# Attention and gated MLP on one core: zero rows under the score operands of the first two pairs of heads

## The chip, the cores and the metric

The kernel runs on one core of a Trainium2 chip. The metric is the time of one execution in device microseconds; a kernel's figure is the median of its runs. The engines are called as the profile calls them: PE (TensorE, its matmuls), PEld (TensorE's weight loads), DVE (VectorE), ACT (ScalarE), POOL (GpSimd), SP (SyncE, whose queue issues nearly all transfers).

## The reference

For 8 batches of 8 heads, with 576 positions and 64 numbers per head, in float32:

```
scores = q @ k^T / 8 + cum[i] - cum[j]     # cum = cumsum(log(clip(f, 1e-4, 1)))
scores = -1e9 above the diagonal
attn   = softmax(scores);  a = attn @ v    # x = heads of a, side by side: 576 x 512 per batch
h      = relu(x @ w_in)                    # 512 -> 1024;  u, v = halves of h
v_n    = layer norm of v over its 512 columns
v_s    = w_spatial @ v_n + b_spatial       # over the 576 positions
out    = (u * v_s) @ w_out                 # 512 -> 512
```

w_in and w_out come as float64, all else as float32.

## The kernel before, in words

Heads are handled in pairs, P = 0 to 31, four pairs to a batch. One pair's attention is: scores, row by row of 128 queries (`scores`, and `scores_tail` for the last 64 queries of both heads); softmax, in which DVE takes the score out of PSUM with the mask and the minimum (L264, L285), ACT takes the exponential (L266, L290), DVE makes the reciprocal of the sums (L269, L270) and POOL multiplies by it (L274, L297); transposes on PE (L320, L333) with a copy out of PSUM; and the product with v (`attend`). The scores of pair P+1 are written between the steps of pair P. After every batch comes its gated MLP (`moe`), interleaved with the attention of later batches.

The scores need q, k and the decay. For the first four pairs (NQ = 4) they are plain float32 products: one tile per head, in the code `ta`, in traces `tf`, of 66 rows by 1216 columns. Columns 0 to 639 are the queries (stationary side), 640 to 1215 the keys (moving side). Rows 0 to 63 are q and k, loaded from memory (L220); rows 64 and 65 are the decay rows, which the kernel computes at its start (`decay_rows`) and copies over by a DMA (L221). There are two such buffers. From pair 4 on, q and k are split in two parts each, in tiles `ta` of 128 rows and `tb` of 68.

At the start PE runs 26 matmuls on `zm[:, 0:128]` and `zm[:, 0:512]`, a part of the mask tile that holds only zeros, into an unused PSUM tile. Meanwhile f is loaded, and DVE, ACT and POOL compute the decay rows (`ft`, `r`, `rt`). Then the weights: `load64` turns float64 into two float32 parts, per piece one ACT operation (L141), five on DVE (L142, L144, L145, L147, L148), two on POOL (L149, L151) and a copy on ACT (L150). `load_first` does four pieces of 512 columns beside the attention of pair 0 and loads w_spatial; `load_rest` does 8 pieces of 256 for w_in, and later 8 for w_out.

The order of each engine's instructions is set at build time by a scheduler that works from the code's order, the dependences and its own costs; each engine and each queue then works strictly in that order. PSUM holds three score tiles (`p0s`) during the first stage.

Of the kernel before, what the change touches and what calls it, by code (L numbers as in the profile page):

```python
# [8 lines left out]
F32 = mybir.dt.float32  # L9
# [9 lines left out]
BIG = 1.0e9  # L19
NF = 5  # L20
NQ = 4
LEAD = 0.25
S = 576
D = 64
# [5 lines left out]
QK = 640 + S  # L30
# [3 lines left out]
def f32(ap):  # L34
    return ap.bitcast(F32)
# [3 lines left out]
def attn_gmlp_kernel(ctx: ExitStack, tc: tile.TileContext, qk, v, f, w_in, w_sp, b_sp, w_out, out):  # L39
# [12 lines left out]
    wk = ctx.enter_context(tc.tile_pool(name="wk", bufs=1))  # L52
# [4 lines left out]
    V, A, G, T, SY = nc.vector, nc.scalar, nc.gpsimd, nc.tensor, nc.sync  # L57
# [139 lines left out]
    def mm(o, l, r, st, sp):  # L197
        T.matmul(o, l, r, start=st, stop=sp)  # L198
# [3 lines left out]
    def split(P):  # L202

        if P < NQ:
            return
# [9 lines left out]
    def prep(P, h):  # L215

        p = slice(64 * h, 64 * h + 64)
        if P < NQ:
            ta = wk.tile([66, QK], F32, name="tf", tag="ta", bufs=2)
            SY.dma_start(out=ta[0:64, :], in_=qk[P, p, :])  # L220
            last['dma', P, h] = SY.dma_start(out=ta[64:66, :], in_=r0s[0][32 * h + P:32 * h + P + 1])  # L221
            tab[P, h] = (ta,)
            return
        hi, lo = parts[P]
        ta = wk.tile([128, QK], F32R, name="ta", tag="ta", bufs=2)
        tb = wk.tile([128, QK], F32R, name="tb", tag="tb", bufs=2)
        SY.dma_start(out=f32(ta[0:64, :]), in_=hi[p, :])
        SY.dma_start(out=f32(ta[64:128, 0:640]), in_=lo[p, 0:640])
        SY.dma_start(out=f32(ta[64:128, 640:QK]), in_=hi[p, 640:QK])
        SY.dma_start(out=f32(tb[0:64, 0:640]), in_=hi[p, 0:640])  # L230
        SY.dma_start(out=f32(tb[0:64, 640:QK]), in_=lo[p, 640:QK])
        SY.dma_start(out=f32(tb[64:68, :]), in_=rows_v[:, P, h, :])
        tab[P, h] = (ta, tb)
# [12 lines left out]
    def qkt(o, P, h, q0, k0, n, first, final):  # L246

        k0 += 640
        ts = tab[P, h]
        for t in ts:  # L250
            r = 66 if len(ts) == 1 else 128 if t is ts[0] else 68
            mm(o, t[0:r, q0:q0 + 128], t[0:r, k0:k0 + n], first and t is ts[0], final and t is ts[-1])

    def scores(P, h):

        nm = wk.tile([128, 4], F32, name="nm", tag="nm", bufs=3)
        sm = wk.tile([128, 4], F32, name="sm", tag="sm", bufs=3)
        for i in range(NB):
            n = 128 * (i + 1)
            q0 = 128 * i  # L260
            sc = PS['s'].tile([128, 512], F32, name="sc")
            qkt(sc[:, 0:n], P, h, q0, 0, n, True, True)
            t = tt[h][:, TOFF[i]:TOFF[i] + n]
            V.tensor_tensor_reduce(out=t, in0=sc[:, 0:n], in1=zm[:, 640 - n:640], scale=-0.125, scalar=3.0e38,  # L264
                                   op0=ALU.add, op1=ALU.min, accum_out=nm[:, i:i + 1])
            last["exp", P, h, i] = A.activation(t, t, AF.Exp, bias=nm[:, i:i + 1], scale=-1.0,  # L266
                                                accum_out=sm[:, i:i + 1])
            yield 2 * max(107, 0.42 * n)
        V.tensor_scalar(out=sm, in0=sm, scalar1=1.0e-9, scalar2=None, op0=ALU.add)  # L269
        V.reciprocal(sm, sm)  # L270
        for i in range(NB):
            n = 128 * (i + 1)
            t = tt[h][:, TOFF[i]:TOFF[i] + n]
            G.tensor_scalar(out=t, in0=t, scalar1=sm[:, i:i + 1], scalar2=1.0, op0=ALU.mult, op1=ALU.mult)  # L274
        yield 0

    def scores_tail(P):
        nm = wk.tile([128, 4], F32, name="nm", tag="nm", bufs=3)
        sm = wk.tile([128, 4], F32, name="sm", tag="sm", bufs=3)
        for j in range(2):  # L280
            k0 = 288 * j
            sc = PS['s'].tile([128, 512], F32, name="sc")
            for h in range(2):
                qkt(sc[:, 0:288], P, h, 512, k0, 288, h == 0, h == 1)
            V.tensor_tensor_reduce(out=tl[:, k0:k0 + 288], in0=sc[:, 0:288],  # L285
                                   in1=zm[:, 0:288] if j == 0 else zm[:, 640:928], scale=-0.125, scalar=3.0e38,
                                   op0=ALU.add, op1=ALU.min, accum_out=nm[:, j:j + 1])
            yield 492
        V.tensor_tensor(out=nm[:, 2:3], in0=nm[:, 0:1], in1=nm[:, 1:2], op=ALU.min)
        A.activation(tl[:, 0:S], tl[:, 0:S], AF.Exp, bias=nm[:, 2:3], scale=-1.0, accum_out=sm[:, 0:1])  # L290
        V.tensor_scalar(out=sm[:, 0:1], in0=sm[:, 0:1], scalar1=1.0e-9, scalar2=None, op0=ALU.add)
        V.reciprocal(sm[:, 0:1], sm[:, 0:1])
        if P >= NF:
            G.tensor_scalar(out=tl[:, S:640], in0=tl[:, TL:S], scalar1=sm[:, 0:1], scalar2=1.0,
                            op0=ALU.mult, op1=ALU.mult)
        if True:
            G.tensor_scalar(out=tl[:, 0:S], in0=tl[:, 0:S], scalar1=sm[:, 0:1], scalar2=1.0,  # L297
                            op0=ALU.mult, op1=ALU.mult)
        yield 0
# [76 lines left out]
    def attention(b, ws=None):  # L376
        for P in range(b * PPB, (b + 1) * PPB):
            if P == 0:
                r0s.append(decay_rows())
                for h in range(2):  # L380
                    prep(0, h)

                warm = ps_a.tile([128, 512], F32, name="x0")
                for _ in range(26):
                    mm(warm, zm[:, 0:128], zm[:, 0:512], True, True)
                split_rows(ws, r0s[0])
                split(1)
                yield from scores(0, 0)
                yield from scores_tail(0)
                yield from scores(0, 1)  # L390
            nxt = P + 1 < NPAIR
            prep_v(P)
            if nxt:
                prep(P + 1, 0)
                prep(P + 1, 1)
# [166 lines left out]
    for b in range(B):  # L562
        gm = moe(b)
        dm, mon = 0.0, True
        while mon:
            while da < min(B, b + 1 + LEAD + dm):
                if not on:
# [46 lines left out]
```

## Time and profile before

| | |
|---|---|
| median of 3 runs | 815.69 us (813.99 to 815.85) |
| profiled execution | 813.26 us, of which the span from the first to the last instruction is 811.5 us |
| mean granted TensorE clock | 0.985 |

A time in the trace is counted from the start of the span. "[2.59 <-DVE nm L264]" behind a row means that the engine sat idle for 2.59 us before it, until DVE's work on `nm` at line 264 was done. "66*128 66x512" on a matmul is the stationary operand (66 rows, 128 columns) and the moving one. A float32 matmul is recorded as two.

### The profile page before, as it was taken

What the parts mean: (1) busy time and instruction counts of PE and PEld (TensorE: products, weight loads), DVE (VectorE), ACT (ScalarE), POOL (GpSimd) and SP (SyncE); (2) the same over time, 40 slices, a digit from 0 to 9 for tenths busy, and PEclk for the clock granted to TensorE, in tenths of its full rate; (3) what the DMA queues carried; (4) which work ended last, traced back from release to release, by engine and by line L of the source; (5) the groups of instructions that cost most, each with busy time, mean ns of one, the idle gap of its engine ahead of it and who ended that gap; (6) DMA issues with size and microseconds to landing.
All of it is one profiled execution on the core that took longest, in us unless ns stands there. A gap on an engine that the chain in (4) does not pass through costs nothing.

```text
span 811.5 us, 15566 instructions
## 1 busy us (share of the span) xinstructions
PE 788.3 (97%) x4980; PEld 704.9 (87%) x4980; DVE 567.1 (70%) x1726; ACT 535.2 (66%) x1432; POOL 478.1 (59%) x677
## 2 busy tenths in 40 slices
PE   7999899999999999999999999999999999999997
PEld 3676678998899989998799989999899988999996
DVE  5879989676976668766776668776786658765321
ACT  5587668676776667666686667776687657764431
POOL 4767788655766647555775537566675547643151
PEclk8699999999999999999999999999999999999999
DMA  7547754456545554565554565556554664430001
GB/s 201 143 121 208 197 140 116 120 151 165 139 122 135 135 146 117 128 166 140 125 141 112 150 152 126 123 144 151 131 130 107 163 164 111 95 77 14 27 1 66
DMA packets 47476, 103.50 MB, mean 128 GB/s; under 512 B 6961, under 2 KB 15153, under 8 KB 47330
## 3 DMA queue, kind: packets, MB, share of 16 engines
q1 hardware_dynamic: 47074, 101.98, 49.8%
q8 instruction: 40, 0.66, 0.3%
q10 hardware_dynamic: 320, 0.52, 0.3%
q14 instruction: 42, 0.34, 0.1%
HBM read 39.41 MB, written 10.68 MB: 62 GB/s over the span
## 4 chain that ended last, share of the span: by engine, by line
PE 87%; DVE 5%; POOL 2%; ACT 2%; DMA 2%; issue 1%; SPq 0%; ACTq 0%; POOLq 0%; DVEq 0%
PE ps L198 47%; PE sc L198 16%; PE x L198 12%; PE tp L320 8%; PE tp L198 2%; PE tp L333 2%; DMA out_dram<-o 1%; POOL tt L274 1%; DVE w L145 1%; ACT tt L266 1%; DVE tt L264 1%; DVE eh L342 0%; DVE wa L142 0%; DVE ef L305 0%; DMA w<-in_dram 0%
## 5 line engine op out<-in xcount | busy, mean ns | idle before, releaser
L274 POOL TENSOR_SCALAR tt<-tt,sm 128x128 f32<-128x128 f32 (+3 forms) x256 | 138.3, 558 | 94.7 <-DVE sm L270 86.4
L264 DVE CUSTOM_DVE_ANT_0 tt<-sc,zm 128x128 f32<-128x128 f32 (+3 forms) x256 | 122.4, 485 | 82.4 <-PE tp L320 63.0
L309 ACT CAST eh<-tp 128x512 fp32r<-128x512 f32 (+1 forms) x270 | 111.5, 425 | 87.2 <-PE tp L320 52.5
L266 ACT ACTIVATE tt<-tt,nm 128x128 f32<-128x128 f32 (+3 forms) x256 | 144.4, 565 | 26.5 <-DVE nm L264 21.5
L310 DVE TENSOR_TENSOR el<-tp,eh 128x512 fp32r<-128x512 f32 (+1 forms) x270 | 127.9, 485 | 25.0 <-ACT eh L309 22.8
L320 PE MATMUL tp<-ident,tt 128*128 128x128 f32 x640 | 113.7, 280 | 1.3 <-DVE ef L305 0.6
L198 PE MATMUL sc<-ta 128*128 128x128 f32 (+1 forms) x336 | 107.8, 327 | 3.9 <-DVE nm L264 3.8
L198 PE MATMUL x<-eh,vt 128*128 128x320 f32 (+4 forms) x378 | 104.5, 287 | 2.7 <-POOL vt L243 1.8
L198 PE MATMUL sc<-tb 68*128 68x128 f32 (+1 forms) x336 | 104.6, 316 | 0.0
L212 POOL TENSOR_TENSOR lo<-raw,hi 128x640 fp32r<-128x640 f32 (+1 forms) x56 | 83.2, 1506 | 18.5 <-ACT hi L210 18.4
L505 POOL TENSOR_TENSOR gl<-u,gh 128x256 fp32r<-128x256 f32 x64 | 47.2, 738 | 79.3 <-ACT gh L504 76.1
L198 PE MATMUL x<-el,vt 128*128 128x256 f32 x324 | 93.4, 306 | 0.0
L320 PEld LDWEIGHTS tp<-ident,tt 128*128 128x128 f32 x640 | 76.8, 142 | 10.9 <-ACT ef L305 1.2
L198 PEld LDWEIGHTS x<-eh,vt 128*128 128x128 f32 x378 | 71.2, 189 | 5.8 <-POOL vt L243 2.7
L198 PE MATMUL ps<-sph,vnh 128*128 128x256 f32 (+1 forms) x240 | 73.3, 306 | 0.2 <-ACT o L530 0.2
L198 PE MATMUL ps<-sph,vnl 128*128 128x256 f32 (+1 forms) x240 | 71.4, 298 | 0.0
L198 PEld LDWEIGHTS sc<-ta 128*128 128x128 f32 x336 | 63.5, 189 | 9.1 <-DVE nm L264 4.9
L198 PE MATMUL ps<-spl,vnh 128*128 128x256 f32 (+1 forms) x240 | 71.2, 296 | 0.0
L198 PE MATMUL ps<-xh,winh 128*128 128x256 f32 (+1 forms) x232 | 70.1, 302 | 0.1
L198 PE MATMUL ps<-xl,winh 128*128 128x256 f32 (+1 forms) x232 | 68.9, 297 | 0.0
L368 ACT CAST xh<-x 64x256 fp32r<-64x256 f32 (+1 forms) x128 | 49.8, 392 | 28.4 <-PE x L198 26.9
L198 PE MATMUL ps<-xh,winl 128*128 128x256 f32 (+1 forms) x232 | 68.4, 295 | 0.0
(190 smaller groups left out, 2127.8 us busy)
## 6 DMA issues: line engine op xcount, KB each, us to landing
raw<-in_dram SPq DMA_DIRECT2D x28, 608.0 KB
ta<-hi SPq DMA_DIRECT2D x56, 304.0 KB
vraw<-in_dram SPq DMA_DIRECT2D x32, 320.0 KB
tb<-hi SPq DMA_DIRECT2D x56, 160.0 KB
ta<-lo SPq DMA_DIRECT2D x56, 160.0 KB
out_dram<-o SPq DMA_DIRECT2D x32, 256.0 KB
ta<-hi SPq DMA_DIRECT2D x56, 144.0 KB
tb<-lo SPq DMA_DIRECT2D x56, 144.0 KB
```

Source lines behind the costliest of these rows:

```text
L145: V.scalar_tensor_tensor(out=w, in0=hi, scalar=0xC0000000, in1=a, op0=ALU.bitwise_and, op1=ALU.bitwise_or)
L198: T.matmul(o, l, r, start=st, stop=sp)
L212: G.tensor_tensor(out=lo[:, c], in0=raw[:, c], in1=f32(hi[:, c]), op=ALU.subtract)
L264: V.tensor_tensor_reduce(out=t, in0=sc[:, 0:n], in1=zm[:, 640 - n:640], scale=-0.125, scalar=3.0e38, op0=ALU.add, op1=ALU.min, accum_out=n ...
L266: last["exp", P, h, i] = A.activation(t, t, AF.Exp, bias=nm[:, i:i + 1], scale=-1.0, accum_out=sm[:, i:i + 1])
L274: G.tensor_scalar(out=t, in0=t, scalar1=sm[:, i:i + 1], scalar2=1.0, op0=ALU.mult, op1=ALU.mult)
L309: A.copy(h_ap, ps)
L310: V.tensor_tensor(out=l_ap, in0=ps, in1=f32(h_ap), op=ALU.subtract)
L320: T.transpose(out=tp[:, (i - c) * 128:(i - c + 1) * 128], in_=tt[h][:, TOFF[i] + 128 * c:TOFF[i] + 128 * c + 128], identity=ident)
L333: T.transpose(out=tp[:, j * 128:(j + 1) * 128], in_=tl[:, c * 128:(c + 1) * 128], identity=ident)
L368: last[P, h] = A.copy(hi, ps[m0:m0 + 64, 0:n])
L505: G.tensor_tensor(out=gl[j][:, 0:256], in0=g[:, 0:256], in1=f32(gh[j][:, 0:256]), op=ALU.subtract)
```

## The change

For pairs 0 and 1 (NPAD = 2) the score tile gets 128 rows in place of 66; DVE sets rows 64 to 127 to zero before the decay rows are copied into 64 and 65, and the matmuls take all 128 rows. Pairs 2 and 3 have 128 rows allotted as well, but use 66 as before.

```diff
+NPAD = 2
...
         if P < NQ:
-            ta = wk.tile([66, QK], F32, name="tf", tag="ta", bufs=2)
+            ta = wk.tile([128, QK], F32, name="tf", tag="ta", bufs=2)
+            if P < NPAD:
+                V.memset(ta[64:128, :], 0.0)
             SY.dma_start(out=ta[0:64, :], in_=qk[P, p, :])
             last['dma', P, h] = SY.dma_start(out=ta[64:66, :], in_=r0s[0][32 * h + P:32 * h + P + 1])
...
         for t in ts:
-            r = 66 if len(ts) == 1 else 128 if t is ts[0] else 68
+            r = (128 if P < NPAD else 66) if len(ts) == 1 else 128 if t is ts[0] else 68
```

Lines of the changed kernel stand one to three higher than before (L264 is L267, L142 is L143). The four memsets change the schedule of the first third of the program; behind about a third of each engine's list the two programs have the same order.

On DVE, at the program's start, before: the decay rows are finished (the scan at L103, the copy at L89), then two operations of the first weight piece come ahead of the first score (L264).

```order
L97 MEMSET ones 64x576
L100 TENSOR_SCALAR ft<-ft 64x576
L85 MEMSET r_114 32x2x64 x2
L103 SCALAR_TENSOR_TENSOR r_114<-ones,ft 64x576
L89 COPY r_114<-r_114 64x512
L85 MEMSET rt 32x4x64 x2
L142 TENSOR_SCALAR wa<-wa 128x512
L144 TENSOR_SCALAR wa<-wa 128x512
L264 ISA tt_94,nm<-sc,zm 128x128
```

The same place in the changed kernel (L104 is the scan, L267 the first score):

```order
L98 MEMSET ones 64x576
L222 MEMSET tf 64x1216 x2
L101 TENSOR_SCALAR ft<-ft 64x576
L86 MEMSET r_114 32x2x64 x2
L86 MEMSET rt 32x4x64 x2
L104 SCALAR_TENSOR_TENSOR r_114<-ones,ft 64x576
L90 COPY r_114<-r_114 64x512
L267 ISA tt_94,nm<-sc,zm 128x128
L267 ISA nm 128x1
L267 ISA tt_94,nm<-sc,zm 128x256
L267 ISA nm 128x1
L143 TENSOR_SCALAR wa<-wa 128x512
```

Two memsets came in behind the first; the memsets of `rt` moved ahead of the scan; and the first two scores moved ahead of the first weight operation, which was ahead of them before.

Further on, on DVE, where the scores of pair 0 end (`tl` is the tail of the queries, `sm` the sums of the softmax, `tt_95` the second head), before:

```order
L285 ISA tl,nm<-sc,zm 128x288
L285 ISA nm 128x1
L285 ISA tl,nm<-sc,zm 128x288
L285 ISA nm 128x1
L264 ISA tt_95,nm<-sc,zm 128x128
L264 ISA nm 128x1
L269 TENSOR_SCALAR sm<-sm 128x4
```

and in the changed kernel:

```order
L288 ISA tl,nm<-sc,zm 128x288
L288 ISA nm 128x1
L148 TENSOR_SCALAR wa<-w_179 128x512
L222 MEMSET tf 64x1216
L272 TENSOR_SCALAR sm<-sm 128x4
L145 TENSOR_SCALAR wa<-wa 128x512
L288 ISA tl,nm<-sc,zm 128x288
L288 ISA nm 128x1
L267 ISA tt_95,nm<-sc,zm 128x128
```

The memset for pair 1's first head and a weight operation now stand between the two halves of the tail. The memset of its second head stands in the same way behind the last score of `tt_95`.

On SP, the transfers for pair 1 and the third and fourth weight piece (`w_342` and `w_410`), before:

```order
L137 DMA w_265<-in_dram 128x1024
L113 DMA rows_d<-rt 64x4864
L232 DMA tb<-rows_d 4x1216
L220 DMA tf<-in_dram 64x1216
L221 DMA tf<-r_114 2x1x1216
L137 DMA w_342<-in_dram 128x1024
L137 DMA w_410<-in_dram 128x1024
L220 DMA tf<-in_dram 64x1216
```

and in the changed kernel (`w_346` and `w_414` are the same two pieces):

```order
L138 DMA w_269<-in_dram 128x1024
L114 DMA rows_d<-rt 64x4864
L223 DMA tf<-in_dram 64x1216
L235 DMA tb<-rows_d 4x1216
L224 DMA tf<-r_114 2x1x1216
L138 DMA w_346<-in_dram 128x1024
L223 DMA tf<-in_dram 64x1216
L224 DMA tf<-r_114 2x1x1216
L138 DMA w_414<-in_dram 128x1024
```

The fourth weight piece moved behind both transfers of pair 1's second head, and each L224 now waits for that buffer's memset, with the weight pieces queued behind it.

## The prediction and its working

> **What bounds the kernel now.** I read the page's engine totals, slices and chain first, then the busy times by stretch, then PE, DVE and SP in order of time over the first 40 us.
>
> ```profile
> span 811.5 us, 15566 instructions
> PE 788.3 (97%) x4980; PEld 704.9 (87%) x4980; DVE 567.1 (70%) x1726; ACT 535.2 (66%) x1432; POOL 478.1 (59%) x677
> ...
> PEclk8699999999999999999999999999999999999999
> ...
> PE 87%; DVE 5%; POOL 2%; ACT 2%; DMA 2%; issue 1%; SPq 0%; ACTq 0%; POOLq 0%; DVEq 0%
> ```
>
> PE is busy for 97% of the span and makes 87% of the chain that ended last. The clock is full but for the first two slices of 20 us, and there lies everything that the change touches.
>
> ```profile
> 10.00:20.00 10.00, 7.41 (x18) 4.48 (x17) 5.88 (x19) 5.20 (x14) 1.80 (x2) 0.62 0.80 217
> 20.00:30.00 10.00, 10.00 (x25) 6.08 (x24) 8.40 (x31) 7.03 (x21) 7.25 (x10) 0.50 0.61 170
> 36.00:40.00 4.00, 3.38 (x18) 2.26 (x17) 3.44 (x13) 1.96 (x5) 2.58 (x3) 0.96 0.69 212
> 40.00:60.00 20.00, 20.00 (x103) 14.76 (x102) 15.39 (x53) 16.24 (x45) 14.16 (x18) 1.00 0.42 117
> 60.00:100.00 40.00, 35.31 (x172) 24.98 (x171) 37.70 (x121) 28.14 (x82) 31.31 (x42) 1.00 0.77 200
> 140.00:811.00 671.00, 661.24 (x4391) 612.62 (x4390) 451.22 (x1386) 442.30 (x1185) 374.91 (x539) 1.00 0.49 121
> ```
>
> The columns are length, then PE, PEld, DVE, ACT, POOL, granted clock. There are four stages: to 36 us PE runs without a pause at half clock; from 40 to 60 it is the bound at full clock while DVE idles 4.6 us; from 60 to 100 DVE is the bound (37.7 of 40); from 140 on PE is at 98.5%. What the first stage gains therefore stays gained if DVE's list too is further along at 60 us: a lead of PE alone would be lost to the third stage.
>
> **Why the clock is low.** The first rows are PEld's and PE's in order of time.
>
> ```profile
> 5.18 0.15 PEld L198 LDWEIGHTS <-zm 128*128 128x128 bf16 x1 [0.28 <-issue]
> 5.60 3.34 PEld L198 LDWEIGHTS <-zm 128*128 128x128 bf16 x16 [0.27 <-issue]
> ...
> 9.61 1.54 PE L198 MATMUL sc<-tf 66*128 66x128 f32 x6 [0.18 <-DMA tf<-r]
> 13.74 11.46 PE L198 MATMUL sc<-tf 66*128 66x512 f32 x22 [2.59 <-DVE nm L264]
> ...
> 28.19 5.75 PE L198 MATMUL sc<-tf 66*128 66x512 f32 x10
> ...
> 33.95 1.06 PE L198 MATMUL x<-ef,vraw 128*128 128x256 f32 x2
> 34.80 1.27 PE L333 MATMUL tp<-ident,tl 128*128 128x128 f32 x5
> 35.87 0.60 PE L198 MATMUL x<-ef,vraw 128*128 128x128 f32 x2
> 36.73 0.63 PE L320 MATMUL tp<-ident,tt 128*128 128x128 f32 x4 [0.26 <-DVE ef L305]
> ```
>
> The weight loads of the opening matmuls start 0.42 us apart until 5.60 and then 0.21 apart (3.34 over 16): all-zero operands of 128 rows brought the clock up within 3.8 us of the first. PE then idles for 2.59 us before 13.74, the clock falls, and through 20 us of unbroken, mostly 66-row matmuls it does not rise; it does at 36.3 (0.96 over the four us from 36), after 2.4 us of 128-row work from 33.95 on. So 66 rows seem not to count as full activity, and zeros do count.
>
> The Trainium skill, page "TensorE: Matmul & The Clock Gate", section "What's actually happening", speaks against the change: the gate opens on how busy PE has recently been, after some 3.4 us of sustained work, and rows are not mentioned. By that alone the clock would have risen near 17 us, and padding would change nothing (the last rival below). Its two states agree with the 0.50 and 1.00 of the rows; the 20 us do not agree with its opening rule.
>
> **The matmuls themselves** cost the same with 128 rows.
>
> ```profile
> 43.86 0.39 PE L198 MATMUL sc<-tf 66*128 66x128 f32 x2
> 44.08 0.39 PE L198 MATMUL x<-ef,vraw 128*128 128x128 f32 x2
> ```
>
> Equal columns, 66 and 128 rows, 0.39 us both: I price the padding on PE at nothing. No instruction is added to PE or SP; four memsets are added to DVE.
>
> **The memsets.** The nearest rows are DVE's memsets at the start, the next rows its pace later.
>
> ```profile
> 0.90 0.54 DVE L97 MEMSET ones<- 64x576 f32 x1 [0.90 <-PEq L600]
> 3.51 0.81 DVE L100 TENSOR_SCALAR ft<-ft 64x576 f32<-64x576 f32 x1 [2.07 <-DMA ft<-in_dram]
> 5.07 1.35 DVE L103 TENSOR_TENSOR_SCAN r<-ones,ft 64x576 f32<-64x576 f32 x1 [0.39 <-ACT ft L101]
> 6.95 0.63 DVE L85 MEMSET rt<- 32x256 f32 x2
> 12.59 0.43 DVE L142 TENSOR_SCALAR wa<-wa 128x512 f32<-128x512 f32 x1 [5.01 <-ACT wa L141]
> ...
> 14.88 0.42 DVE L147 TENSOR_SCALAR wa<-w 128x512 uint32<-128x512 uint32 x1
> 15.22 0.55 DVE L264 CUSTOM_DVE_ANT_0 tt<-sc,zm 128x384 f32<-128x384 f32 x1
> ...
> 16.03 0.68 DVE L264 CUSTOM_DVE_ANT_0 tt<-sc,zm 128x512 f32<-128x512 f32 x1
> ...
> 16.64 0.69 DVE L148 SCALAR_TENSOR_TENSOR wa<-w,wa 128x512 f32<-128x512 uint32 x1
> 17.24 0.68 DVE L145 SCALAR_TENSOR_TENSOR w<-w,wa 128x512 uint32<-128x512 uint32 x1
> ...
> 34.74 1.64 DVE L148 SCALAR_TENSOR_TENSOR wa<-w,wa 128x512 f32<-128x512 uint32 x1
> ```
>
> 256 elements take 0.315 us and 576 take 0.54, so 1216 take 1.0 at that slope, 1.14 in proportion; I take 1.05. The two memsets of pair 0 run from 1.44 to 3.54, inside the 2.07 us in which DVE waits for f. If f came sooner they would cost up to 2.1. What does cost is the reordering behind them: the memsets of `rt` now precede the scan and need POOL's memset of `rt`.
>
> ```profile
> 3.96 1.47 POOL L82 MEMSET rt<- 64x1280 f32 x1
> ```
>
> That ends at 5.43, so the scan starts near 6.06 instead of 5.07. The decay rows, the first score (9.61) and, behind the decay rows on SP, the first weight load come 1.0 us later.
>
> The two memsets of pair 1 stand in DVE's list where it is busy: 2.1 us. Had they the stretch that a two-source operation shows (1.64 for 0.69), they would cost up to 5.0; at least 2.0.
>
> **The first stage, as DVE's list.** The mark is the copy and the score (L305, L264) that DVE reaches at 36.51, behind which PE starts its transposes at 36.73. From 13.39 to 36.51 are 23.1 us. Nominal cost by start-to-start distances in the rows above: 11 scores 4.3 (0.61 for 512, 0.47 for 384, down to 0.21), two tails 0.8, 10 one-source weight operations at 0.34 = 3.4, 8 two-source ones at 0.60 = 4.8, copies 0.7, small ones 0.7: 14.7. Of the rest, 4.3 are waits and 4.1 are operations that took longer than nominal.
>
> ```profile
> DVE tl L285 <- PE sc L198: 1.5, 1, 1.5
> ...
> DVE w L145 <- POOL winl L151: 1.1, 1, 1.1
> DVE tt L264 <- PE sc L198: 0.9, 1, 0.9
> ...
> DVE wa L142 <- POOL w L149: 0.6, 1, 0.6
> ```
>
> 2.4 of the waits are for PE at half clock, 1.7 for POOL.
>
> In the changed order, the first two scores leave PSUM before the weight piece arrives, so the 2.59 us gap of PE goes. DVE's dense work starts when ACT has the first piece:
>
> ```profile
> 11.90 0.66 ACT L141 ACTIVATE wa<-w 128x512 f32<-128x512 f32 x1 [1.14 <-DMA w<-in_dram]
> ...
> 20.26 2.69 SPq L137 DMA_DIRECT2D w<-in_dram  x2
> ...
> 21.65 2.48 POOL L274 TENSOR_SCALAR tt<-tt,sm 128x128 f32<-128x128 f32 x4 [0.61 <-DVE sm L270]
> ```
>
> 11.90 + 1.0 for the later load and 0.66 on ACT is 13.55. Up to the same mark the list lacks the first two scores (-0.55) and six weight operations, three of each kind, which the scheduler put behind it (-2.8); it has one L143 more (+0.35) and the two memsets (+2.1): 14.7 - 0.9 = 13.8 nominal, to 27.4. With all 4.1 us of stretch, 31.5; with POOL's waits of 1.7 as well, 33.2. PE's waits I take as gone, up to a rest: the memset in the tail leaves PE some 2 us without work near 17 to 19, the clock can fall again there, and then needs some 3 us of 128-row work to return. I set that at 0.3, since the most stretched weight operations are among the six put off. The mark comes at 33.5, which is 3.0 us earlier. The 2.8 us put off fall into the 4.6 us that DVE idles from 40 to 60, and cost nothing; were that cover gone, the gain would be 0.2.
>
> POOL does not overturn this: its multiplications start no earlier than 21.65 (the sums stand behind the memset), but its fourth weight sum (L149) also moved behind those of pair 1. SP's third weight load goes out when its buffer is free, near 20 us as before (20.26); the row copy ahead of it waits for a memset that ends near 18.
>
> PE at 36 us has 22.7 busy us at half clock, 11.3 of work at full. It can shed up to 11 us of busy time; 3.0 come off the end, the rest turns into waits for DVE.
>
> **Sum.** 813.26 - 3.0 = 810.3 for a profiled execution. That one stands 2.4 below the median, so the median goes from 815.69 to 812.7. Bounds: no waits at all and half the stretch gives a gain of 36.5 - 29.5 = 7.0, 808.7; all 4.3 of waits returned gives 33.5 + 2.4 = 35.9, a gain of 0.6, 815.1.
>
> **The rivals.**
> - The gain is eaten: DVE waits as long as before, now on POOL and ACT, and PE's freed time is idle. For it: POOL's multiplications start no earlier. Gain about 0.5: 815.2.
> - Slower: the memsets of pair 1. DVE reaches each while PE still reads the buffer, waits, then takes up to 2.5 us; behind it stand the sums that release POOL, and on SP the decay rows and a weight load. Price 5.0 at most and 2.1 at least, plus the 1.0 at the start, middle 4.5; it decides once PE's faster clock returns less than the price. With a return of 0.9: 819.3. Against it: 2432 columns at 0.22 us per 128 (43.86 to 44.08) are 4.2 us, which with a wait of 0.6 for a free PSUM tile frees pair 0's first buffer at 15.4; DVE gets to the memset near 17.
> - The clock does not answer to padding. PE then starts 1.6 us earlier (no wait at 13.74) at half rate, gaining perhaps 1.5 from the clock held until its next pause, and loses 2.9 on the memsets: gain 0.2, 815.5.
> - More: few waits left, gain 6.0: 809.7.
>
> **Numbers.** A measurement of this kernel can tell about 0.3%, 2.4 us, from no change. Chances: the forecast 0.45 (three quarters of it beyond 2.4 us), more 0.10, eaten 0.20, no answer of the clock 0.10, slower 0.15. Faster 0.33 + 0.10 = 0.43; same 0.12 + 0.20 + 0.10 = 0.42; slower 0.15. The range, 808.7 to 817.5, holds all but the slower case; the forecast alone is 810.5 to 814.5.
>
> **What would show it.** The idle before the fourth score is gone; the clock at 20 to 30 us lies well above 0.50; PE is no longer 100% busy there and waits for DVE; the transposes of 36.73 start near 33.7; the memsets take about 1.05 us; the six weight operations run between 35 and 60 us at no cost to PE. Wrong: a clock at 0.50 until the 128-row products, DVE waiting for PE ahead of a memset, or a start at 33.7 that is lost again by 140 us.

## The result, and the profile after

The changed kernel takes 819.66 us (median of 5, 818.39 to 821.01); the kernel before took 814.38 beside it (813.99 to 815.85). The ratio is 1.0059, with a 95% interval of 1.0046 to 1.0072: the change makes the kernel slower by 5.3 us (4.8 by the ratio), where 812.7 was forecast in a range of 808.7 to 817.5. The profiled execution of the changed kernel has a span of 816.7 us. Its totals and slices:

```profile
span 816.7 us, 15552 instructions
...
PE 784.4 (96%) x4980; PEld 702.9 (86%) x4980; DVE 574.3 (70%) x1730; ACT 535.5 (66%) x1432; POOL 480.9 (59%) x677
...
PEclk9999999999999999999999999999999999999999
```

PE's clock is now 0.9 or more in every slice, and PE is busy 3.9 us less; yet the span is 5.2 us longer. So the clock came, and PE's time went into waiting. Stretches that the prediction read (length, PE, PEld, DVE, ACT, POOL, granted clock, DMA share, GB/s), in the changed kernel:

```profile
20.00:30.00 10.00, 9.02 (x33) 5.41 (x32) 9.53 (x28) 7.00 (x22) 8.34 (x10) 0.83 0.51 155
36.00:40.00 4.00, 2.83 (x11) 1.51 (x10) 4.00 (x14) 3.15 (x10) 2.66 (x3) 1.00 0.20 44
40.00:60.00 20.00, 19.70 (x92) 14.39 (x92) 14.89 (x47) 15.02 (x40) 15.76 (x20) 0.91 0.37 105
140.00:811.00 671.00, 665.95 (x4421) 617.80 (x4420) 456.59 (x1395) 444.69 (x1192) 378.23 (x542) 1.00 0.48 120
```

From 20 to 30 us the clock is 0.83 where it was 0.50. But from 36 to 40 DVE has no free moment (4.00) and PE is idle 1.17 us; from 40 to 60 the clock is 0.91 where it was 1.00. The last row looks better than before (PE 665.95 against 661.24), but only because work that was done ahead of 140 us now stands behind it. The same by larger stretches, first the kernel before:

```profile
0.00:36.00 36.00, 31.44 (x84) 18.29 (x85) 23.07 (x62) 18.32 (x43) 22.18 (x34) 0.67 0.63 170
36.00:60.00 24.00, 23.38 (x119) 17.02 (x118) 18.82 (x65) 18.20 (x50) 16.74 (x20) 0.99 0.46 132
100.00:145.00 45.00, 41.93 (x260) 36.88 (x259) 41.17 (x110) 30.61 (x79) 37.52 (x50) 1.00 0.55 136
145.00:200.00 55.00, 53.95 (x362) 50.11 (x360) 37.88 (x123) 36.82 (x104) 28.00 (x42) 1.00 0.54 139
```

and the changed kernel:

```profile
0.00:36.00 36.00, 28.64 (x111) 16.39 (x112) 28.70 (x75) 19.71 (x48) 22.72 (x34) 0.95 0.69 194
36.00:60.00 24.00, 22.53 (x103) 15.89 (x102) 18.89 (x60) 18.17 (x49) 18.43 (x22) 0.93 0.34 95
60.00:100.00 40.00, 32.60 (x165) 24.06 (x165) 35.45 (x112) 26.28 (x75) 30.13 (x41) 1.00 0.82 198
100.00:145.00 45.00, 39.42 (x217) 33.71 (x216) 39.03 (x104) 29.08 (x75) 35.08 (x45) 0.92 0.48 126
145.00:200.00 55.00, 55.00 (x381) 51.98 (x380) 39.16 (x126) 36.77 (x104) 31.93 (x48) 1.00 0.56 140
```

PE's busy time multiplied by the granted clock is, roughly, the work that it did. To 36 us that is 27.2 after (28.64 x 0.95) against 21.1 before (31.44 x 0.67): 6.1 us gained. From 36 to 60 it is 21.0 against 23.1, from 60 to 100 32.6 against 35.3 (the row of the prediction), from 100 to 145 36.3 against 41.9: 10.4 lost, and 1.0 won back by 200 us. That leaves the changed kernel some 3.4 us behind; the rest of the 5.2 us of span comes later. The gain of the first stage was twice what was forecast, and all of it was lost, and more, between 36 and 145 us. From 100 to 145 us, where most was lost, the rows name two parts: 2.5 us less of busy time (39.42 for 41.93), and a clock of 0.92 where it was 1.00, which is 3.2 us of PE's work (39.42 x 0.08).

### The profile page after: what moved, and what is told of

Same layout as the page of the kernel before. It is cut to its first block, busy times and chain, and to the rows that moved or that the text cites. A ratio compares the mean times of both kernels' runs of the same rounds, so it can differ in the third digit from the quotient of the medians.

```text
span 816.7 us, 15552 instructions
## 1 busy us (share of the span) xinstructions
PE 784.4 (96%) x4980; PEld 702.9 (86%) x4980; DVE 574.3 (70%) x1730; ACT 535.5 (66%) x1432; POOL 480.9 (59%) x677
## 4 chain that ended last, share of the span: by engine, by line
PE 78%; DVE 2%; ACT 1%; POOL 1%; issue 1%; DMA 0%; POOLq 0%; ACTq 0%
PE ps L199 44%; PE sc L199 13%; PE x L199 10%; PE tp L323 7%; PE tp L199 2%; PE tp L336 2%; DVE vx L459 0%; DVE wa L149 0%; DVE el L313 0%; POOL vt L246 0%; DMA out_dram<-o 0%; DVE eh L345 0%; ACT eh L312 0%; POOL tt L277 0%; ACT vt L245 0%
## 5 line engine op out<-in xcount | busy, mean ns | idle before, releaser
L267 DVE CUSTOM_DVE_ANT_0 tt<-sc,zm 128x128 f32<-128x128 f32 (+3 forms) x256 | 122.2, 485 | 85.6 <-PE tp L323 60.0
L313 DVE TENSOR_TENSOR el<-tp,eh 128x512 fp32r<-128x512 f32 (+1 forms) x270 | 127.5, 484 | 23.1 <-ACT eh L312 21.0
```

Of the source, the lines that this page charges most:

```text
L313: V.tensor_tensor(out=l_ap, in0=ps, in1=f32(h_ap), op=ALU.subtract)
```

## The experiments

Each group of runs stands beside runs of the kernel before, whose median was 813.95 to 815.30 from group to group; so differences of under 1.5 us between runs of different groups are read by the ratios.

In many of them each engine and each queue is held to an order of choice. A table gives for every engine the order of its instructions, and each instruction depends on the one ahead of it (a cut from the code; memsets that a run adds stay outside of the table):

```diff
+    for e, ranks in table.items():
+        mine = per[e]
...
+        for a, b in zip(ranks, ranks[1:]):
+            tc.add_manual_dep(mine[b], mine[a].name, info, reason="order")
```

The changed kernel held to its own order is the same program, instruction for instruction, so the method costs nothing by itself.

**What the padding is worth in one order.** For e1 to e3 pair 1 uses the two score tiles of pair 0, so the zeros are set once and two memsets, at the start, are enough; the three have the same order. e1 uses 66 rows in all matmuls, e2 128 rows in pairs 0 and 1, e3 in all four pairs. e4 has the change's four memsets and 66 rows, in an order that is again its own.

```diff
-            ta = wk.tile([128, QK], F32, name="tf", tag="ta", bufs=2)
-            if P < NPAD:
+            ta = tab[0, h][0] if 0 < P < NPAD else wk.tile([128, QK], F32, name="tf", tag="ta", bufs=2)
+            if P == 0:
                 V.memset(ta[64:128, :], 0.0)
```

> Two memsets instead of four: pair 1 reuses pair 0's two buffers, whose rows 66 to 127 stay zero. All scores take 66 rows. Its order of instructions is its own (neither that of before nor of the changed kernel), and the same as that of e2 and e3. If the padding itself makes the time (through the clock), this one runs like the kernel before, 814 to 815 us, with a clock of 0.50 somewhere between 15 and 36 us, and e2 and e3 differ from it. If the memsets of pair 1 make it, it is within 1 us of the kernel before, as e2 and e3 are. If the new order of the first third makes it, all three share one time, which may be anything from 811 to 820.

> As e1, with pairs 0 and 1 at 128 rows: the change with two memsets less, in the order of e1. Padding theory: 3 to 5 us away from e1, clock near 1.0 between 20 and 36 us. Memset theory: at least 3 us faster than the changed kernel, within 1 us of e1. Order theory: within 1 us of e1, whatever the clock does before 36 us.

> As e2, with all four float32 pairs at 128 rows, in the order of e1. Padding theory: further in the direction of e2 against e1, since pairs 2 and 3 cover 40 to 75 us. Order and memset theories: within 1 us of e1 and e2.

> The four memsets of the change, all scores at 66 rows; its order is again its own. Padding theory: about 814 to 815, as before, clock at 0.50 for most of 20 to 36 us. Memset theory: 818 to 820, as the changed kernel. Order theory: a time unlike that of the changed kernel, for instance within 2 us of before.

Measured, with before at 814.71: e1 819.19 (ratio 1.0056, 1.0044 to 1.0068), e2 815.15 (1.0007, 0.9999 to 1.0016), e3 815.12 (1.0006, 0.9997 to 1.0014), e4 822.20 (1.0100, 1.0078 to 1.0123). The stretches from 20 to 36 us, of e1:

```profile
20.00:30.00 10.00, 9.70 (x23) 5.56 (x22) 6.88 (x22) 7.67 (x22) 7.26 (x10) 0.50 0.51 156
30.00:36.00 6.00, 6.00 (x27) 4.79 (x26) 4.08 (x15) 1.91 (x5) 3.43 (x5) 0.66 0.57 142
```

and of e2:

```profile
20.00:30.00 10.00, 7.82 (x33) 5.59 (x33) 7.66 (x24) 8.05 (x23) 8.52 (x12) 0.83 0.52 155
30.00:36.00 6.00, 6.00 (x32) 4.41 (x32) 6.00 (x22) 3.62 (x12) 3.62 (x4) 1.00 0.64 201
```

At equal order the rows of zeros bring the clock from 0.50 to 0.83, and 4.0 us at the end (e1 to e2). So the reason that the prediction gave for the slow clock is right: the rows in use decide, and rows of zeros count. Pairs 2 and 3 add nothing (e3): by then the clock is up. But e1 shows something that was not looked for: nothing but two memsets at the start and another order, and 4.5 us lost, where 814 to 815 was expected if the padding made the time. e4 came out above everything that was expected of it, and its order differs from all the others, so it separates nothing.

**Order, memsets and padding apart.** e5 is the kernel before, without a memset, in the changed kernel's order; e7 adds the four memsets to it. e6 is the whole change in the order of before; e8 is e2 in that order, e9 is e8 with 66 rows.

> The kernel before, unchanged in its work (66 rows, no memset), with each engine held to the order that the changed kernel has. Order theory: this order alone costs, 821 to 824 us. Memset theory: the order is harmless and the memsets of pair 1 cost, so within 1 us of before. The first stage should lose the gap of 2.59 us on PE in either.

> The whole change (four memsets, pairs 0 and 1 at 128 rows) with each engine held to the order of the kernel before, the memsets alone coming in between. Order theory: padding's 4 us come through, 810 to 812 us. Memset theory: 818 to 820, as the changed kernel. Middle: 813 to 815 if the memsets of pair 1 cost what the padding brings.

> The changed kernel in its own order with all scores back at 66 rows, memsets kept. If padding brings 4 us in this order as it does between e1 and e2: 823 to 824 us. If the gain of the first stage is lost again later in this order whatever the rows: 819 to 820. Clock 0.50 for most of 20 to 36 us.

> Pairs 0 and 1 at 128 rows, two memsets at the start only, order of the kernel before. Order theory: 810 to 812 us, as e6 or up to 2 us faster. Memset theory: 810 to 812 too, and 7 us or more faster than e6. If padding is worth nothing in this order: 814 to 815.

> Two memsets at the start, all matmuls at 66 rows, every engine held to the order of the kernel before; it is e8_once_pad2_old_order (815.7) without the padding. Theory 'another chain sets the end of the first stage in the old order' (in e8 PE ran at full clock from 24 to 32 us, then sat idle for 4.87 us until DVE came to its copy at 36.74, which it does 0.4 us later than in the kernel before at half clock): the padding is worth nothing there, the extra is the 1.0 us of the memsets at the start: 814.5 to 816.0, and PE without a long pause before 37. Rival 'padding is worth 4 us in any order, and something else in e8 costs 5.7': 818.5 to 820.5.

Measured, with before at 813.95: e5 818.99 (1.0068, 1.0054 to 1.0082), e6 816.19 (1.0030, 1.0018 to 1.0042), e7 821.82 (1.0098, 1.0085 to 1.0111), e8 815.70 (1.0022, 1.0012 to 1.0031); with before at 814.28, e9 815.48 (1.0017, 1.0006 to 1.0027). In the changed order, then: the order alone costs 5.0 us, the memsets 2.8 more (e7 less e5), and the padding gives 2.2 back (819.66 less 821.82; 3.2 by the ratios). In the order of before the two memsets of pair 1 cost 0.5 us (e6 less e8). The order theory is right for e5, though less than its 821 to 824 came of it, and wrong for e6 and e8, where the padding's 4 us were to come through (810 to 812). e7 lies between its two ranges, and e9 where the theory of another chain put it.

In the order of before the padding gives nothing (e8 against e9), although the clock is up there too (in e8 0.83 from 20 to 30 us and 1.00 from 30 to 36). Why shows in the rows of DVE's copy, first of e8 with 128 rows, then of e9 with 66:

```profile
36.74 0.28 DVE L308 COPY ef<-tp 128x128 f32<-128x128 f32 x1
```

```profile
36.52 0.28 DVE L308 COPY ef<-tp 128x128 f32<-128x128 f32 x1
```

and of PE, which needs the copy, of e8:

```profile
31.91 0.39 PE L199 MATMUL x<-ef,vraw 128*128 128x128 f32 x2
37.16 0.83 PE L323 MATMUL tp<-ident,tt 128*128 128x128 f32 x4 [4.87 <-DVE ef L308]
```

and of e9:

```profile
36.70 0.63 PE L199 MATMUL x<-ef,vraw 128*128 128x128 f32 x2
37.12 0.77 PE L323 MATMUL tp<-ident,tt 128*128 128x128 f32 x4
```

DVE comes to the copy at the same time, whatever PE's clock. In e9 it waits 1.4 and 0.8 us for PE's scores on the way; in e8 these waits are gone, and a longer one stands in the list of weight operations, beside 1.16 us for POOL ahead of 32.95:

```profile
26.41 0.43 DVE L143 TENSOR_SCALAR wa<-wa 128x512 f32<-128x512 f32 x1 [2.67 <-POOL tl L300]
```

By the row this wait is for POOL (26.39); ACT's step on the same weight piece, which had waited 1.89 us for the transfer, ended at 26.30, so the transfer may have set it as well. In either case it was not PE that DVE waited for. PE at full clock is done at 32 us and waits 4.87; at half clock it is done just as the copy comes. So PE's 100% of 20 to 36 us was a coincidence of two limits, and a faster PE moves only its own idle time. In the changed order DVE's list no longer ends there, since weight operations were put off; there the faster clock shows (2.2 us), as it does in the order of e1 and e2 (4.0).

**Where behind the first stage the time goes.** e12 is the whole change in the changed kernel's order up to where it stood at 90 us, and in that of before from there on.

> The whole change (four memsets, pairs 0 and 1 padded): each engine in the changed kernel's order up to where it stood at 90 us, in the order of the kernel before from there on. The changed kernel's PE led by 1.3 to 2.0 us there. Theory 'the later order loses the lead': 811.5 to 813.5. Rival 'the lead is PE's alone, and DVE's list, longer by four memsets, has it back by 140 us in any order': 815 to 817. That the order after 90 us has nothing to do with it: 819 to 820.5.

Measured 815.55 (1.0015, 1.0005 to 1.0025), in the range of the rival: 4.1 us less than the changed kernel (819.66 less 815.55; 3.6 by the ratios) for another order behind 90 us, far from the memsets. It does not keep the lead either: in its profiled execution (817.18, among the longest of its runs) PE waits 2.80 us for DVE ahead of 94.54, just behind the joint. Three attempts were made to find one place there. In the changed kernel DVE spends 3.53 us on a weight operation that takes 0.42 at 105.68, and the next score stands behind it. DVE:

```profile
105.68 0.42 DVE L149 SCALAR_TENSOR_TENSOR wa<-w,wa 128x256 f32<-128x256 uint32 x1
...
135.23 3.53 DVE L149 SCALAR_TENSOR_TENSOR wa<-w,wa 128x256 f32<-128x256 uint32 x1
138.68 0.54 DVE L267 CUSTOM_DVE_ANT_0 tt<-sc,zm 128x384 f32<-128x384 f32 x1
```

POOL works beside it:

```profile
135.57 2.90 POOL L213 TENSOR_TENSOR lo<-raw,hi 128x640 fp32r<-128x640 f32 x2
```

and PE waits for the score:

```profile
139.28 0.40 PE L199 MATMUL sc<-ta 128*128 128x288 f32 x1 [2.52 <-DVE nm L267]
```

The Trainium skill, page "GPSIMD Engine Reference", section "8. Key points", says that POOL shares its memory interfaces with DVE, and that they contend where DVE's instruction has two inputs from memory; this operation has two, and it ends (138.76) within 0.3 us of POOL's (138.47). That POOL is the reason is a reading of these rows, not shown by a run. In e13 that operation stands behind the two scores; in e10 a weight load stands ahead of six copies on SP's queue; e14 has e13's move and SP's queue in the order of before from the 51st transfer on.

```diff
 DVE, e13:
-SCALAR_TENSOR_TENSOR wa<-w,wa 128x256      (L149)
 the scores tt<-sc,zm 128x384 and 128x512, vx<-vx,mv
+SCALAR_TENSOR_TENSOR wa<-w,wa 128x256
 SP, e10:
 DMA w<-in_dram 128x4x128
+DMA w<-in_dram 128x4x128
 DMA ta<-hi, ta<-lo, ta<-hi, tb<-hi, tb<-lo, tb<-rows_d
-DMA w<-in_dram 128x4x128
```

> The whole change in its own order (819.66), but one weight load (the second of those that run near 91 to 99 us) is put on SP's queue directly behind the first, ahead of six copies of operands, as the kernel before has it. Theory 'the lead is lost to that load': ACT's wait for it (3.38 us before 102.00) and DVE's (4.73 us before 102.47) shrink by some 3 us, the lead at 110 us grows by as much, and 2 to 3 us of it reach the end: 816.5 to 818. Rival 'lost to POOL's stretch of DVE at 135 us and the falls of the clock, whatever comes ahead': 819 to 820.5. Slower than that would mean that the copies, now behind the load, are what PE needs.

> The whole change in its own order (819.66), but on DVE one weight operation (L149, which took 3.53 us from 135.23) stands behind the two scores that it was ahead of. Theory 'that place gives the lead back': PE's 2.52 us of idle before 139.28 goes, and with it the fall of the clock from 140 to 143 (0.70 over 140 to 145: 1.5 us): 815.7 to 817.5. Rival 'the weight pieces are what the end waits for, wherever the operation stands' or 'another wait takes its place': 819 to 820.5.

> As e13_score_first, and SP's queue in the order of the kernel before from the 51st transfer on (two weight loads ahead of six copies at 91 us, in place of one, and the one that ACT wants last first). ACT's wait of 3.38 us and DVE's of 4.73 before 102.47 should go. Theory 'both places matter': 1 to 2.5 us below e13: 813.5 to 816. Rival 'the loads do not matter' (as e10, 819.16, had it for one of them): within 0.7 of e13.

Measured: e10 819.16 (1.0056, 1.0040 to 1.0073); with before at 815.30, e13 819.08 (1.0055, 1.0041 to 1.0068) and e14 821.47 (1.0068, 1.0050 to 1.0085); the changed kernel has 1.0059. None brings anything back. For e10 and e13 the rivals' ranges hold; e14 was to lie within 0.7 us of e13 by its rival and lies 2.4 above it by the medians, 1.1 by the ratios, whose intervals overlap. PE's longest waits from 100 to 145 us (for whom, us in total, times, longest), in the changed kernel:

```profile
PE sc L199 <- DVE nm L267: 2.5, 1, 2.5
...
PE ps L199 <- DVE vx L453: 1.0, 1, 1.0
```

and in e13:

```profile
PE ps L199 <- DVE vx L453: 2.2, 1, 2.2
...
PE sc L199 <- DVE nm L288: 0.6, 1, 0.6
```

The wait of 2.5 us is gone as meant, but PE waits 2.2 in place of 1.0 for DVE some us ahead of the moved operation, and 0.6 behind it. What stands ahead of the move can't be its consequence: it shows that the waits of this stretch are not the same from run to run, while the time comes out the same. The moved operation took 0.41 us at its new place; beside POOL's two operations stood `vx<-vx,mv` now, and it took 1.93 us where the changed kernel has 0.69.

**Can e2's lead be kept?** By matmuls counted in stretches of 4 us, PE in e2 stands about 5 us ahead of the kernel before at 99 us, and about 1 behind at 140. e11 and e15 are e2 with the order of before from about 95 and 88 us on, e15 with SP's queue in that order from the 51st transfer on.

> Two memsets, pairs 0 and 1 padded, as e2_once_pad2 (815.15): each engine in e2's order up to where e2 stood at 95 us, and in the order of the kernel before from there on. e2's PE led by 5.3 us at 98 us (matmuls counted) and had lost all of it by 140. Theory 'the later order loses the lead, and the order of before would keep it': 809 to 811, faster than the kernel before by 3 to 5 us. Rival 'DVE and POOL have that work to do in either order and the lead of PE is not a lead of theirs': 814 to 815.5.

> Two memsets, pairs 0 and 1 padded, as e2_once_pad2 (815.15), each engine in the order of the kernel before from where e2 stood at 88 us on, SP's queue already from its 51st transfer (some 62 us). In e11 ACT waited 6.21 us for a weight load that stood behind another in the queue; here the loads come in the order in which ACT takes them. Theory 'the lead of 5 us at 98 us reaches the end if the loads are in time': 809.5 to 812. Rival 'DVE and POOL have the same work to do by 140 us, and the lead is PE's alone': 814 to 816.

Measured: e11 816.29 (1.0017, 1.0006 to 1.0029), e15 817.28 (1.0024, 1.0013 to 1.0035). Both are worse than e2 (1.0007), and above both ranges that were expected of them. DVE in e11:

```profile
101.58 0.29 DVE L143 TENSOR_SCALAR wa<-wa 128x256 f32<-128x256 f32 x1 [5.36 <-ACT wa L142]
```

and PE in e15:

```profile
84.58 0.58 PE L199 MATMUL sc<-ta 128*128 128x288 f32 x1 [5.12 <-DMA ta<-hi]
```

In e11 the lead ended at a weight load that stood late in the queue (DVE waited 5.36 us for ACT, and ACT for the load; PE then 2.73 for a copy by ACT); in e15, with the weight loads early, at the score operands behind them (PE waited 5.12). The mixtures made these waits themselves, so they don't show that no order keeps the lead; they show that a lead of PE does not carry the transfers with it. Whether another order would keep it is open.

**Is it DVE and POOL?** e16 to e18 leave out the low words of the last 16 weight pieces, in before, e2 and the changed kernel, each in its own order (a shortened cut):

```diff
-        V.tensor_scalar(out=a, in0=w, scalar1=0xFF800000, ...)
-        V.scalar_tensor_tensor(out=af, in0=lo, scalar=2.0 ** -52, in1=af, ...)
-        G.tensor_tensor(out=wf, in0=wf, in1=af, op=ALU.add)
+        if mark:                 # only in the first four pieces
+            (the same three)
```

> The kernel before, in its own order, without the low words of the last 16 weight pieces (L147, L148 on DVE, L149 on POOL): some 11 us less on DVE (16 times 0.28 + 0.41) and 11.7 us less on POOL (16 times 0.73) between 58 and 145 us; these outputs lack that part. PE's idle there was 4.7 us at 60 to 100, 1.1 at 115 to 125 and 2.0 at 125 to 140. If DVE and POOL are what PE waits for there: 808 to 811. If transfers are: 813 to 815.

> e2_once_pad2 (two memsets, pairs 0 and 1 padded, 815.15) without the same 48 operations, in its own order. Theory 'the lead of 5 us is lost to DVE and POOL': with them relieved it stays, 3 to 5 us below e16. Rival 'lost to the transfers and the order': within 1 us of e16, as e2 is of before (+0.4).

> The whole change in its own order (819.66) without the same 48 operations. Theory 'lost to DVE and POOL': the 5.9 us by which its first stage ends earlier, less the 1.0 to 2.5 that it loses ahead of 60 us, stay: 2 to 4 us below e16. Rival 'lost to the transfers and the order': 3 to 5 us above e16, as the changed kernel is above before (+5.3).

Measured, with before at 814.35: e16 811.87 (0.9970, 0.9957 to 0.9982), e17 808.88 (0.9929, 0.9917 to 0.9942), e18 814.31 (1.0004, 0.9992 to 1.0017). In e16, from 60 to 100 us, DVE's busy time falls from 37.70 to 31.70 and POOL's from 31.31 to 24.10, with the transfers as before:

```profile
60.00:100.00 40.00, 35.53 (x172) 26.92 (x171) 31.70 (x103) 28.12 (x81) 24.10 (x34) 0.91 0.81 196
```

With DVE and POOL relieved, e2's version is 3.0 us faster than before's (with the full work 0.4 slower), and the changed kernel is 2.4 us slower (5.3). So about 3 us of either lead are lost with that work in place. One caution: in the profiled executions the clock from 60 to 100 us is 0.91 in e16, 0.96 in e17 and 0.91 in e18, so a part of e17's 3.0 us can be the clock. The other 2.4 us of the changed kernel remain when the work is light (e18 lies between its two expected ranges, e16 just above 808 to 811). What is left there are its order, its memsets and the transfers; no run separates them, and no single place was found. That half is open.

No version that does the full work was faster than the kernel before; e2 and e3 equal it.

## Why the prediction was wrong, point by point

The steps of the first stage, in the changed kernel, PE:

```profile
10.58 3.37 PE L199 MATMUL sc<-tf 128*128 128x128 f32 x12 [0.71 <-DMA tf<-r]
14.79 1.46 PE L199 MATMUL sc<-tf 128*128 128x288 f32 x6 [0.85 <-DVE nm L267]
17.05 0.70 PE L199 MATMUL sc<-tf 128*128 128x256 f32 x2 [0.80 <-DVE nm L288]
19.68 4.31 PE L199 MATMUL sc<-tf 128*128 128x384 f32 x8 [1.92 <-DVE nm L288]
...
30.84 0.52 PE L323 MATMUL tp<-ident,tt 128*128 128x128 f32 x3
...
40.30 0.44 PE L323 MATMUL tp<-ident,tt 128*128 128x128 f32 x2 [1.12 <-POOL tt L277]
```

and DVE:

```profile
6.54 1.35 DVE L104 TENSOR_TENSOR_SCAN r<-ones,ft 64x576 f32<-64x576 f32 x1
...
17.65 1.07 DVE L222 MEMSET tf<- 64x1216 f32 x1 [0.31 <-issue]
...
30.42 0.27 DVE L308 COPY ef<-tp 128x128 f32<-128x128 f32 x1
...
31.22 0.93 DVE L149 SCALAR_TENSOR_TENSOR wa<-w,wa 128x512 f32<-128x512 uint32 x1
...
39.22 0.67 DVE L149 SCALAR_TENSOR_TENSOR wa<-w,wa 128x512 f32<-128x512 uint32 x1
```

- **The clock and the zeros: right**, and shown by e1 and e2 at equal order. The rule of the Trainium skill that the prediction weighed (page "TensorE: Matmul & The Clock Gate", section "What's actually happening") would have had no difference between them; the measured 0.50 and 0.83 decide.
- **The memsets: right in size** (1.05 forecast, 1.07 measured), and DVE did not wait long ahead of them (0.31). The first score came 1.0 us later, as forecast (10.58 for 9.61); the scan came 1.5 later, not 1.0: the two memsets at the start ran to 4.08, not 3.54, and the operation on f behind them took 1.32 us for 0.81. The gap of 2.59 us is gone; PE's pauses behind it are there, and the clock fell after the third.
- **The mark: mis-sized.** DVE's copy and PE's transposes came at 30.42 and 30.84, 5.9 us earlier, where 3.0 was forecast. The sum kept nearly all of the list's waits and stretches; but the most stretched operations were among those put off. The range for this step (up to 7.0) held it.
- **The six weight operations put off: the first step that failed.** They were to fall into DVE's idle time from 40 to 60 us and cost nothing. They ran from 31.22 to 39.89 (the first and the last of the six are shown), took 4.1 us from start to start in place of 2.8, and DVE had no free moment from 36 to 40. PE waited 1.12 us ahead of 40.30, by its row for POOL's product, and POOL had waited for DVE's reciprocal of the sums (L273), ahead of which one of the six stands at 37.16:

```profile
38.02 3.45 POOL L277 TENSOR_SCALAR tt<-tt,sm 128x128 f32<-128x128 f32 x4 [1.34 <-DVE sm L273]
```

  Then the clock fell:

```profile
42.00:44.00 2.00, 2.00 (x5) 1.28 (x4) 1.21 (x2) 1.88 (x6) 2.00 (x3) 0.50 0.00 0
```

  By 60 us some 2 us of the lead were gone, as the stretches above have it.
- **"What the first stage gains stays gained if DVE's list too is further along at 60 us": the step that decided.** The prediction followed the new order only as far as 36 us and gave everything behind it no cost; measured alone (e5), the order costs 5.0 us. Nor was the condition tested against the new order, in which the list was not further along. POOL's fourth and last weight sums, first in the kernel before:

```profile
36.46 1.27 POOL L149 TENSOR_TENSOR w<-w,wa 128x512 f32<-128x512 f32 x1 [0.63 <-DVE wa L148]
...
77.00 0.90 POOL L149 TENSOR_TENSOR w<-w,wa 128x256 f32<-128x256 f32 x1
...
142.34 0.74 POOL L149 TENSOR_TENSOR w<-w,wa 128x256 f32<-128x256 f32 x1 [0.36 <-DVE sm L269]
```

  and in the changed kernel:

```profile
42.16 1.27 POOL L150 TENSOR_TENSOR w<-w,wa 128x512 f32<-128x512 f32 x1
...
77.83 0.73 POOL L150 TENSOR_TENSOR w<-w,wa 128x256 f32<-128x256 f32 x1
...
150.41 0.74 POOL L150 TENSOR_TENSOR w<-w,wa 128x256 f32<-128x256 f32 x1 [0.77 <-DVE wa L149]
```

  It is 5.7 us behind at the fourth piece, 1.4 at the fifth (64.55 for 63.16), only 0.8 at the eighth, and 8.1 at the last: the first lag was nearly made good, and a new one opened behind 78 us. That the lag of this list makes the loss is not shown, and being ahead was not enough. In e2 the fifth sum comes 1.8 us earlier than in the kernel before (61.33 for 63.16), so there the condition is met at 60 us; the lead lasts past 100 us and is lost by 140 all the same. And e2's last sum,

```profile
151.64 0.74 POOL L150 TENSOR_TENSOR w<-w,wa 128x256 f32<-128x256 f32 x1 [3.09 <-DVE wa L149]
```

  comes 9.3 us late, while e2 takes the time of the kernel before. What in the order costs the 5.0 us stays open.
- **PE as the limit of the first stage: wrong in a way that the trace of before could not show.** Its rows had PE busy without a pause from 20 to 36 us. e8 and e9 show that DVE's list, with POOL and the weight pieces, ended at the same time.
- **The rivals.** "Slower" gave 819.3 and had the measured time with another cause: it priced the memsets, with the later start, at 4.5 us, and all four cost 2.8 (e7 less e5). That its number was so near is luck. "Eaten" had the mechanism of DVE waiting on, but in the first stage, where the lead in fact came. A new order that costs by itself was no rival, and the prediction's own last sign of error ("a start at 33.7 that is lost again by 140 us") was what happened, with a start at 30.84.

## What to carry to other kernels

A change that makes a scheduler write another order is two changes; follow the new order as far as it differs, and ask of every engine, not of the fastest one, whether it is further along at the end of each stage; e2 shows that even this need not be enough. An engine that is busy without a pause need not be the limit: where another list ends at the same moment, speeding the one up only turns its work into waiting. If a change's mechanism works and the time gets worse, run the old work in the new order: it is one run, and it told more here than any row of the trace.

## What was not expected of the hardware

- Short pauses were followed by falls of the clock. In the changed kernel 1.17 us of idle within 36 to 40 us were followed by a clock of 0.50 from 42 to 44. The section of the Trainium skill named above gives one idle window of about 3.4 us for that; no single pause there was longer than 1.12 us. It happened twice more behind single pauses: 0.50 from 120 to 122 us behind the one below, and 0.50 from 140 to 142 behind the 2.52 us ahead of 139.28.

```profile
118.81 0.57 PE L199 MATMUL ps<-winh,xh 128*128 128x512 f32 x1 [1.26 <-ACT vx L454]
```

- A DVE operation of two inputs, 0.42 us long at another place, took 3.53 us beside two of POOL's; taking it out of PE's way (e13) changed the time by nothing that can be told.
